# Lead-in of a fused retention and feed-forward kernel: k and q of units 1 to 3 loaded ahead of their V, V of units 1 and 2 scaled by GpSimd, tail tables made by products on VectorE

## The chip, the cores and the metric

The kernel runs on one core of a Trainium2 chip. The metric is the device time of one execution in microseconds (us); lower is better. Most executions of one kernel agree within about 0.3%, which is 0.9 us here.

TensorE is called PE below (the weight loads that overlap it PEld), VectorE is DVE, ScalarE is ACT, GpSimd is POOL. "L454" is line 454 of the kernel. The changed set-up functions are one line longer in all, so the lines after them (from L302 on) have a number one higher: L454 of the kernel before is L455 of the changed kernel. Some experiments shift them a little further.

## The reference, cut to what matters

```python
# q, k, v: (8 batches, 8 heads, 576 positions, 64), float32
scores = (q @ k.T) / sqrt(64)
gamma  = 1 - 2 ** (-5 - head)                 # one decay per head
ret    = scores * where(i >= j, gamma ** (i - j), 0)
x      = (ret @ v)  -> (4608, 512)            # heads side by side
h      = x @ w_in                             # (512, 2048)
out    = (h * sigmoid(1.702 * h)) @ w_out     # (2048, 512)
```

The kernel cuts the 4608 rows into 36 units of 128 rows. The decay `gamma ** (i - j)` is split into a factor of the row of q (table `gq`, applied when the result leaves PSUM, the memory that TensorE writes to) and a factor of the row of V (table `vfac`, applied to V before use). Earlier blocks of one batch enter through a running state (`kv`). For each unit TensorE transposes k and q and makes the scores; VectorE masks them (`pm`); "inter" is q times the running state, "values" the masked scores times the scaled V (`vp`), and both add up to the product that VectorE multiplies by `gq` into `xT`. Four units make one chunk of 512 rows for the feed-forward products. Unit 8 of each pair of batches holds both batches' last 64 rows ("tail") and needs its own rows of the two tables.

## The kernel before

Each engine has its own list of operations; a scheduler class puts in semaphore waits where one engine reads what another wrote. So the order of the calls below is the order on each engine. The first four units are written out by hand; this is the lead-in, which ends with the first up-projection (`up(0, 0)`, L454).

```python
def scale_v(u):                       # V times its decay factor, on VectorE
    sl, _, ty = u % NVN, *unit_info(u)[1:]
    op("dve", lambda e: e.tensor_tensor(
        vp[u % NVP].ap(), vn[sl].ap(),
        vfac[:, ty, :, None].to_broadcast([P, H, DH]), ALU.mult), ...)

def setup_last():                     # tables of the tail, as exponentials on ScalarE
    for hp in range(HP):
        op("act", ... gq[:, 4, hp, :] = Exp(iota_c[512:576] * lng + lnsc))
    # ... two small additions on VectorE ...
    for h in range(H):
        op("act", ... vfac[:, 4, h] = Exp(-log(gamma(h)) * iota_t))

# ... the lead-in ...
for i, src in enumerate((k, q)):      # unit 0: SyncE's queue
    op("sp", ... kq32[:, i, :] <- src[0, :, 0:P, :])
load_v(0, "sp")
setup_first(); setup_gq(0, 1); setup_gq(1, 4); setup_last()
for u in range(1, 4):                 # GpSimd's queue, in this order
    load_kq(u)                        # k, then q; float32 in DRAM, bf16 in SBUF
    load_v(u)                         # float32 to float32
for i in range(4):
    load_win(i)                       # w_in: 4 blocks, each 1 MB in DRAM
for u in range(4, 8):
    load_kq(u)
    load_v(u)
# ...
warm(10)                              # filler matmuls that keep PE busy
transpose_half(0, 0, "S2", "dve"); transpose_half(0, 1, "S3", "dve")
warm(3)
head_s(0)                             # scores on PE, two mask products on VectorE
scale_v(0); scale_v(1)
transpose_half(1, 0, "S2", "act")     # PE transposes k of unit 1, ScalarE copies
warm(4)
transpose_half(1, 1, "H0", "act")
head_k(0, "act")                      # state: PE, then two copies on ScalarE
head_v(0)                             # inter + values on PE, product xT on VectorE
head_s(1)
scale_v(2)
# ... unit 2 ...
head_k(1, "act"); head_s(2); scale_v(3); head_v(1)
# ... unit 3 ...
head_k(2, "act"); setup_gelu(); head_s(3); head_v(2); warm(3); head_v(3)
head_k(3, "act"); setup_tail()
warm(2)
play(16, lambda f: up(0, f), {9: [lambda: head_in(4, "dve")], ...})
```

`up(0, f)` reads `xT` of units 0 to 3 and block `f // 4` of `w_in`. `head_in(4)`, after ten of the sixteen up-projections, transposes k and q of unit 4.

## Time and profile before

| | |
|---|---|
| time, median of 3 runs | 312.8 us (312.46 to 312.85) |
| span of the profiled run | 311.03 us |
| PE busy | 301.9 us, 97% |
| first up-projection (L454) | starts at 19.72 us |
| last load of the lead-in (V of unit 3) | lands at 15.95 us |

The page of the profile first gives the busy time of each engine, and then slices of 1/40 of the span in tenths:

```profile
PE 301.9 (97%) x2169; PEld 155.7 (50%) x2169; DVE 134.5 (43%) x272; ACT 123.4 (40%) x225; POOL 105.6 (34%) x132
PE   6799999999999999999999999999999999999994
```

PE is full in all slices but the first two (15.5 us) and the last. The busy times of the other engines, 34 to 43%, say nothing of use: they are averages over stages. What can be gained is the time until the first up-projection, so one reads the chain of waits there. The chain is followed back from the last instruction; each line is a start, a length and what ran; "issue" is time for which the profile shows no wait, and `psS`, `psO`, `psH` are banks of PSUM. This is its part in the lead-in (cuts marked by dots):

```profile
7.16 1.70 POOL kq L203 x2
8.86 7.09 DMA vn<-in_v_dram
15.95 0.02 issue
15.98 0.69 DVE vp L302
16.67 0.60 DVE xT L443
17.27 0.60 DVE pm_0 L423
17.87 0.61 DVE pm_1 L423
18.48 0.04 issue
18.52 0.41 PE psO L433 x7
18.93 0.33 PE psS L347 x4
...
19.72 8.81 PE psH L454 x40
```

GpSimd issues loads (L203), the V of unit 3, issued at 8.86, lands at 15.95, then VectorE scales it (`vp`), finishes unit 1 (`xT`) and masks the scores of unit 3 (`pm`), then PE does the values of unit 3. The chain leaves one thing out. L454 also reads `xT`, and VectorE's timeline has the last two `xT` products end at 18.38 + 1.28 = 19.66, 0.06 before L454:

```profile
18.38 1.28 DVE L443 TENSOR_TENSOR xT<-psO,gq 128x512 bf16<-128x512 f32 x2
```

The chain follows PE's own earlier instructions there, because fillers kept PE from being idle.

### The profile page before, as it was taken

To read this page: it belongs to the slowest core of one execution; us is meant where nothing else is said; L and a number is where in the kernel's file an instruction comes from. 1 tells how busy PE (TensorE), PEld (TensorE's weight loads), DVE (VectorE), ACT (ScalarE), POOL (GpSimd) and SP (SyncE) were. 2 spreads that over 40 slices of the span, in tenths; PEclk is the share of its full clock that TensorE was granted. 3 is DMA by queue.
4 is the path that set the end of the run, shared out by engine and by line. 5 is a ranking of instruction groups with operands and counts; after the bars stand their busy time and mean duration, and the time that the engine had idled before them with its cause. 6 is when DMAs were issued, how large, how long until landed. Compare 5 with 4: busy or idle time off the path is not lost.

```text
span 311.0 us, 5149 instructions
## 1 busy us (share of the span) xinstructions
PE 301.9 (97%) x2169; PEld 155.7 (50%) x2169; DVE 134.5 (43%) x272; ACT 123.4 (40%) x225; POOL 105.6 (34%) x132
## 2 busy tenths in 40 slices
PE   6799999999999999999999999999999999999994
PEld 2444588655454545454545454545454545444441
DVE  5761984597445542545363625362627150100000
ACT  9666345301433333333333333333343434343411
POOL 9999923015699935334454300000000000000000
PEclk9999999999999999999999999999999999999999
DMA  9999999999999999999999999923210102010012
GB/s 150 184 207 188 190 203 175 176 187 157 182 118 200 168 163 150 170 135 176 179 141 190 145 148 182 142 47 86 45 68 2 67 2 67 2 67 34 36 67 67
DMA packets 113752, 39.40 MB, mean 127 GB/s; under 512 B 102785, under 2 KB 106881, under 8 KB 113729
## 3 DMA queue, kind: packets, MB, share of 16 engines
q0 software_dynamic: 80016, 22.55, 74.7%
q1 hardware_dynamic: 33712, 16.52, 30.9%
q8 instruction: 17, 0.28, 0.4%
q14 instruction: 7, 0.05, 0.1%
HBM read 36.70 MB, written 9.44 MB: 148 GB/s over the span
## 4 chain that ended last, share of the span: by engine, by line
PE 92%; POOL 3%; DMA 2%; DVE 2%; ACT 0%; issue 0%; POOLq 0%
PE psH L454 36%; PE psS L485 33%; PE psH L471 5%; PE psH L485 5%; PE psO L433 3%; PE psS L414 3%; DMA vn<-in_v_dram 2%; PE psS L347 2%; PE psO L485 2%; POOL kq L203 2%; PE psO L395 1%; PE psS L311 1%; POOL vn L217 1%; DVE vp L302 0%; DVE xT L443 0%; DVE pm_0 L423 0%
## 5 line engine op out<-in xcount | busy, mean ns | idle before, releaser
L454 PE MATMUL psH<-xT,w_in_sb 128*128 128x512 bf16 x512 | 127.3, 380 | 0.0
L459 ACT ACTIVATE gT<-psH 128x512 bf16<-128x512 f32 x128 | 76.4, 597 | 116.1 <-PE psH L454 116.1
L485 PE MATMUL psS<-w_out_sb,gT 128*128 128x512 bf16 x480 | 117.3, 379 | 0.0
L454 PEld LDWEIGHTS psH<-xT,w_in_sb 128*128 128x128 bf16 x512 | 47.8, 98 | 58.7 <-ACT gT L459 3.2
L485 PEld LDWEIGHTS psS<-w_out_sb,gT 128*128 128x128 bf16 x480 | 46.0, 98 | 51.7
L203 POOL DMA_DIRECT2D kq<-in_k_dram x39 | 35.6, 921 | 43.3 <-DMA qkT<-kq 22.7
L203 POOL DMA_DIRECT2D kq<-in_q_dram x39 | 35.5, 919 | 15.2 <-issue 15.2
L217 POOL DMA_DIRECT2D vn<-in_v_dram x39 | 36.0, 932 | 9.3 <-issue 5.0
L423 DVE TENSOR_TENSOR pm_0<-psS,mask 128x512 bf16<-128x512 f32 x32 | 22.0, 687 | 37.6 <-PE psS L414 37.5
L493 ACT ACTIVATE osb<-psS 128x512 f32<-128x512 f32 x30 | 17.9, 597 | 30.4 <-PE psS L485 30.4
L443 DVE TENSOR_TENSOR xT<-psO,gq 128x512 bf16<-128x512 f32 x36 | 23.5, 682 | 11.4 <-PE psO L433 11.4
L302 DVE TENSOR_TENSOR vp<-vn,vfac 128x512 bf16<-128x512 f32 x36 | 23.7, 685 | 2.6 <-DMA vn<-in_v_dram 2.5
L423 DVE TENSOR_TENSOR pm_1<-psS,mask 128x512 bf16<-128x512 f32 x32 | 21.8, 680 | 0.0
L377 DVE TENSOR_TENSOR kvf<-psS,kvf 64x256 f32<-64x256 f32 x24 | 10.1, 421 | 26.2 <-PE psS L347 26.0
L471 PE MATMUL psH<-xT,w_in_sb 128*128 128x256 bf16 x128 | 15.2, 273 | 0.0
L485 PE MATMUL psH<-w_out_sb,gT 128*128 128x512 bf16 x64 | 15.0, 380 | 0.0
L476 ACT ACTIVATE gT<-psH 128x512 bf16<-128x512 f32 x16 | 9.6, 597 | 11.5 <-PE psH L471 11.5
L414 PE MATMUL psS<-qkT 64*128 64x128 bf16 x288 | 12.2, 218 | 1.1 <-ACT qkT L330 0.9
L433 PE MATMUL psO<-pm_0,vp 128*64 128x128 bf16 x144 | 13.1, 224 | 0.0
L433 PE MATMUL psO<-pm_1,vp 128*64 128x128 bf16 x144 | 12.5, 223 | 0.5 <-DVE pm_1 L423 0.5
L471 PEld LDWEIGHTS psH<-xT,w_in_sb 128*128 128x128 bf16 x128 | 12.0, 98 | 1.9 <-issue 0.2
L375 DVE COPY kvf<-psS 64x256 f32<-64x256 f32 x12 | 5.0, 420 | 18.2 <-PE psS L347 18.1
(78 smaller groups left out, 171.9 us busy)
## 6 DMA issues: line engine op xcount, KB each, us to landing
out_dram<-osb SPq DMA_DIRECT2D x32, 256.0 KB, 3.1
vn<-in_v_dram POOLq DMA_DIRECT2D x31, 256.0 KB, 20.0
kq<-in_k_dram POOLq DMA_DIRECT2D x31, 128.0 KB, 21.4
kq<-in_q_dram POOLq DMA_DIRECT2D x31, 128.0 KB, 21.3
w_in_sb<-in_moe_w_in_dram POOLq DMA_DIRECT2D x4, 512.0 KB, 11.2
w_out_sb<-in_moe_w_out_dram POOLq DMA_DIRECT2D x4, 512.0 KB, 19.6
vn<-in_v_dram POOLq DMA_DIRECT2D x8, 128.0 KB, 23.1
out_dram<-osb SPq DMA_DIRECT2D x8, 128.0 KB, 4.3
```

Of the source, the lines that this page charges most:

```text
L203: e.dma_start(kq[sl][p0 : p0 + n, i, :].rearrange("p (h d) -> p h d", d=DH), src[b, :, s0 : s0 + n, :].rearrange("h p d -> p h d"),)
L217: e.dma_start(vn[sl][p0 : p0 + n, :, :], v[b, :, s0 : s0 + n, :].rearrange("h p d -> p h d"),)
L302: op("dve", lambda e: e.tensor_tensor(vp[u % NVP].ap(), vn[sl].ap(), vfac[:, ty, :, None].to_broadcast([P, H, DH]), ALU.mult), reads=[f"vn ...
L414: op("pe", lambda e, hp=hp, hh=hh, bank=bank: e.matmul(by_pair(bank)[:, hp, :], qt[64 * hh : 64 * hh + 64, hp, :], qt[64 * hh : 64 * hh + ...
L423: op("dve", lambda e: e.tensor_tensor(pm[u % 4][hh].ap(), by_pair(bank), m[:, None, :].to_broadcast([P, HP, P]), ALU.mult), reads=[bank, " ...
L433: op("pe", lambda e, hp=hp, hh=hh: e.matmul(ob[64 * hh : 64 * hh + 64, hp, :], vp[u % NVP][:, 2 * hp + hh, :], pm[u % 4][hh][:, hp, :], st ...
L443: op("dve", lambda e: e.tensor_tensor(xT[ch % 3][:, :, 128 * j : 128 * j + 128], by_pair(bank), gq[:, ty, :, :], ALU.mult), reads=[bank] + ...
L454: op("pe", lambda e, a=a: e.matmul(hb, w_in_sb[:, a, P * f : P * f + P], xT[c % 3][:, a, :], start=(a == 0), stop=(a == HP - 1)), reads=[f ...
L459: op("act", lambda e: e.activation(gT[c % 2][:, f, :], hb, AF.Gelu_apprx_sigmoid), reads=[bank], writes=[f"gT{c % 2}_{f}"])
L471: op("pe", lambda e, a=a, f=f, j=j: e.matmul(hb[:, j, :], w_in_sb[:, a, P * f : P * f + P], xT[c % 3][:, a, n], start=(a == 0), stop=(a == ...
L485: op("pe", lambda e, f=f: e.matmul(y, gT[c % 2][:, f, P * r : P * r + P], w_out_sb[:, f, :], start=(f == 0), stop=(f == NF - 1)), reads=[f ...
L493: op("act", lambda e: e.activation(osb[o].ap(), y, AF.Copy), reads=[bank], writes=[f"osb{o}"])
```

## The change

The intent is to shorten the lead-in: have the transposes and scores of units 1 to 3 done earlier by loading their k and q first, take two products off VectorE, which is on the chain, and take twelve exponentials off ScalarE. The diff, cut:

```diff
-        def setup_last():            # ... 12 exponentials on ScalarE, 2 additions ...
+        def setup_g64():
+            op("act", ... g64 = Exp(64 * lng))
         def setup_tail():
             ...
+            op("dve", ... gq[:, 4] = gq[:, 3, :, 64:128] * g64)
+            for h in range(H):
+                for hh in range(2):
+                    op("dve", ... vfac[64*hh : 64*hh+64, 4, h] =
+                              vfac[64*hh : 64*hh+64, 3, h] * gamma(h) ** (64.0*hh - 128.0))
-        def scale_v(u):
+        def scale_v(u, eng="dve"):
-        setup_last()
-        for u in range(1, 4):
-            load_kq(u)
-            load_v(u)
-        for i in range(4):
-            load_win(i)
+        setup_g64()
+        load_kq(1)
+        load_kq(2)
+        load_v(1)
+        load_kq(3)
+        load_v(2)
+        load_v(3)
+        load_win(0)
+        load_win(1)
+        scale_v(1, "pool")
+        load_win(2)
+        scale_v(2, "pool")
+        load_win(3)
@@ order of the lead-in's work, the new order from unit 1 on @@
+        head_v(0)
+        transpose_half(2, 0, "S2", "act")
+        head_s(1)
+        transpose_half(2, 1, "H0", "act")
+        head_k(0, "act")
+        warm(1)
+        head_s(2)
+        transpose_half(3, 0, "S2", "act")
+        inter(1); values(1); values_out(1)
+        transpose_half(3, 1, "H0", "act")
+        head_k(1, "act")
+        warm(1)
+        head_s(3)
+        scale_v(3)
+        warm(2)
+        head_k(2, "act")
+        head_v(2)
+        setup_gelu()
+        inter(3); values(3); values_out(3)
+        head_k(3, "act")
+        setup_tail()
```

More of the change, by code (lines that the diff above doesn't have):

```diff
@@ L167, in bass_retnet_parallel__then__act_gelu_quick_kernel @@
         iota_k = sb("iota_k", [P, 4], FP32)
-        iota_t = sb("iota_t", [P, 1], FP32)
+        g64 = sb("g64", [P, HP], FP32)
         scr = sb("scr", [P, 1], FP32)
@@ L268, in setup_gq @@
                    writes=[f"gq{hp}_{c}" for c in range(c0, c1)])
-        def setup_last():
-            for hp in range(HP):
-                op("act", lambda e, hp=hp: e.activation(
-                    gq[:, 4, hp, :].rearrange("p (t i) -> p t i", i=64),
-                    iota_c[:, None, 512:576].to_broadcast([P, 2, 64]),
-                    AF.Exp, bias=lnsc.ap(), scale=lng[:, hp : hp + 1]),
-                   reads=["iota_c", "lnsc", f"lng{hp}_0", f"lng{hp}_1"], writes=[f"gq{hp}_4"])
-            op("dve", lambda e: e.tensor_scalar_add(iota_t[0:64], iota_k[0:64, 0:1], 512.0),
-               reads=["iota_k"], writes=["iota_t0"])
-            op("dve", lambda e: e.tensor_scalar_add(iota_t[64:128], iota_k[64:128, 0:1], 448.0),
-               reads=["iota_k"], writes=["iota_t1"])
-            for h in range(H):
-                op("act", lambda e, h=h: e.activation(
-                    vfac[:, 4, h : h + 1], iota_t.ap(), AF.Exp, scale=-math.log(gamma(h))),
-                   reads=["iota_t0", "iota_t1"], writes=[f"vfact{h}"])
+        def setup_g64():
+            op("act", lambda e: e.activation(g64.ap(), lng.ap(), AF.Exp, scale=64.0),
+               reads=[f"lng{hp}_{hh}" for hp in range(HP) for hh in range(2)], writes=["g64"])
         def setup_gelu():
@@ L295, in setup_tail @@
                 op("dve", lambda e, j=j: e.memset(kv[1][j].ap(), 0.0), writes=[f"kv1_{j}"])
+            op("dve", lambda e: e.tensor_tensor(
+                gq[:, 4, :, :].rearrange("p a (t i) -> p a t i", i=64),
+                gq[:, 3, :, None, 64:128].to_broadcast([P, HP, 2, 64]),
+                g64[:, :, None, None].to_broadcast([P, HP, 2, 64]), ALU.mult),
+               reads=["g64"] + [f"gq{hp}_3" for hp in range(HP)],
+               writes=[f"gq{hp}_4" for hp in range(HP)])
+            for h in range(H):
+                for hh in range(2):
+                    op("dve", lambda e, h=h, hh=hh: e.tensor_single_scalar(
+                        vfac[64 * hh : 64 * hh + 64, 4, h : h + 1],
+                        vfac[64 * hh : 64 * hh + 64, 3, h : h + 1],
+                        gamma(h) ** (64.0 * hh - 128.0), ALU.mult),
+                       reads=[f"vfac{h}"], writes=[f"vfact{h}_{hh}"])
         VF = [f"vfac{h}" for h in range(H)]
-        VFT = [f"vfact{h}" for h in range(H)]
-        def scale_v(u):
+        VFT = [f"vfact{h}_{hh}" for h in range(H) for hh in range(2)]
+        def scale_v(u, eng="dve"):
             sl, _, ty = u % NVN, *unit_info(u)[1:]
-            op("dve", lambda e: e.tensor_tensor(
+            op(eng, lambda e: e.tensor_tensor(
                 vp[u % NVP].ap(), vn[sl].ap(),
@@ L630, in bass_retnet_parallel__then__act_gelu_quick_kernel @@
         scale_v(0)
-        scale_v(1)
         transpose_half(1, 0, "S2", "act")
@@ L634, in bass_retnet_parallel__then__act_gelu_quick_kernel @@
         transpose_half(1, 1, "H0", "act")
+        head_v(0)
+        transpose_half(2, 0, "S2", "act")
+        head_s(1)
+        transpose_half(2, 1, "H0", "act")
         head_k(0, "act")
-        head_v(0)
-        head_s(1)
-        scale_v(2)
-        transpose_half(2, 0, "S2", "act")
-        warm(2)
-        transpose_half(2, 1, "H0", "act")
-        head_k(1, "act")
-        head_s(2)
-        scale_v(3)
-        head_v(1)
-        transpose_half(3, 0, "S2", "act")
-        transpose_half(3, 1, "H0", "act")
+        warm(1)
+        head_s(2)
+        transpose_half(3, 0, "S2", "act")
+        inter(1)
+        values(1)
+        values_out(1)
+        transpose_half(3, 1, "H0", "act")
[3 more added lines that the diff above has]
+        scale_v(3)
+        warm(2)
         head_k(2, "act")
+        head_v(2)
         setup_gelu()
-        head_s(3)
-        head_v(2)
-        warm(3)
-        head_v(3)
+        inter(3)
+        values(3)
+        values_out(3)
         head_k(3, "act")
```

## The prediction

> **What bounds it now.** The page gives TensorE (PE) 301.9 of 311.0 us (97%); the chain that ended last is 92% PE. From 20 us on PE is nearly full (windows: 2.00 of 2.00 us in each from 20 to 36). PE work is unchanged but for fewer filler matmuls, so only the lead-in can change: the time to the first up-projection (L454) at 19.72 us (PE timeline). The chain there: GpSimd issues loads back to back (0.88 us each), V of unit 3 lands at 15.95, then four VectorE ops of 0.6 us (scale V 3, xT of unit 1, two mask products of unit 3), then values, states and filler on PE.
>
> **What the change does.**
> - Load order. Landings (semaphores): k1 7.73, q1 9.03, v1 10.32, k2 11.20, q2 12.04, v2 13.33, k3 14.21, q3 15.04, v3 15.95. A k or q costs about 0.86, a V 1.3. In the new order: k2 9.9, q2 10.8, v1 12.0, k3 12.9, q3 13.8, v2 15.0, v3 still about 16.0, as the bytes are the same.
> - V of units 1 and 2 leave VectorE (0.69 us each). On GpSimd, an estimate from the Trainium skill (GPSIMD Engine Reference, Performance versus the Vector engine: a 2048-wide tensor_tensor 4497 ns, VectorE 2293): about 1.2 us for 512. They hold GpSimd's queue, so w_in 2 and 3 and all after are issued up to 4.5 us later; but the queue is 14 us deep there (w_in 3 issued 11.95, landed 25.88), so landings should not move.
> - ScalarE loses 12 exponentials (L272 1.63 us, L282 0.84 us), gains one: the first kT copy goes at 8.2 instead of 9.02. Not on the chain, which waits for loads.
> - VectorE gains one 128x512 product and 16 tiny ones (about 2 us) after the last xT, where it idles 7.9 us. Free.
>
> **New chain.** v2 lands 15.0; GpSimd to 16.3; state 2 on PE to 16.65; its ScalarE copies (0.76) to 17.45; inter and values of unit 3 to 18.1; xT 3 on VectorE to 18.8; first L454 at 18.9. The mask products of unit 3 and xT 1 are done before. Gain at L454 about 0.8 us, out of the 3.8 us that followed v3.
>
> **What caps it.** Unit 4's transposes come 8.6 us after the first L454. q4 landed 27.76 and is used at 28.58: slack 0.8 us, so more gain than that is lost there. The first w_in block (18.18) has 0.7 us.
>
> **Prediction.** 312.8 - 0.7 = 312.1 us, 8 in 10 between 311.5 and 312.7. Faster by over 2%: 0.01; within 2%: 0.97; slower by over 2%: 0.02.
>
> **What would show it.** First L454 near 18.9; v2 landing near 15.0, v3 near 16.0; GpSimd TENSOR_TENSOR near 1.2 us; the chain of waits in the lead-in passing through GpSimd's product of unit 2 and the kv_2 copy instead of VectorE's mask products; q4 landing still near 27.8, with a short PE wait at unit 4's transposes; everything after shifted alike.
>
> **What would make it wrong.** A GpSimd product of 2 us eats the gain one for one. VectorE and GpSimd contending: the skill (SBUF — State Buffer, Who interferes with whom) says a VectorE op with two SBUF inputs and a GpSimd op that reads SBUF block each other; scale V 3 starts about when the second product ends. Late issue of w_in 3 leaving a hole in the load queue would move every later landing. Fewer fillers might let the PE clock drop (granted 1.00 now).

## More of the kernel before

The runs were made in four sessions; in each, the kernel before was run beside the others on the same chip, and times are only compared within a session.

## The result, and the profile after

Ratios are the mean time of one kernel's runs over that of the other's runs of the same rounds, so they are not quite the ratio of the medians that are quoted beside them.

| | before | changed |
|---|---|---|
| median of 5 runs | 312.85 us (312.46 to 313.25) | 312.69 us (312.36 to 313.00) |
| ratio | | 0.9994 (95%: 0.998 to 1.0007) |
| span of the profiled run | 311.03 | 310.65 |
| first up-projection | 19.72 | 19.33 |

The time lies in the predicted range (311.5 to 312.7) at its upper edge, and the ratio by itself doesn't tell a gain from none. The profile tells more. These are the same lines of the page:

```profile
PE 302.3 (97%) x2168; PEld 155.9 (50%) x2168; DVE 136.6 (44%) x285; ACT 121.6 (39%) x214; POOL 108.1 (35%) x134
PE   7799999999999999999999999999999999999994
```

And this is the chain of waits in the lead-in:

```profile
8.08 7.21 DMA vn<-in_v_dram
15.29 0.08 issue
15.37 1.04 POOL vp L303
16.41 0.14 issue
16.55 0.40 PE psS L348 x4
...
16.97 0.38 ACT kv_2 L361
...
17.36 0.39 ACT kv_2 L361
...
17.80 0.40 PE psO L396 x4
18.19 0.34 PE psO L434 x8
18.54 0.33 PE psS L348 x4
...
19.33 8.81 PE psH L455 x40
```

The chain is the one that the prediction wrote down: V of unit 2 lands, GpSimd multiplies it, PE makes the state, ScalarE copies it in two pieces, PE does inter and values of unit 3. VectorE's `xT` of unit 3, 18.58 to 19.27, again stands beside the last PE lines:

```profile
18.58 0.69 DVE L444 TENSOR_TENSOR xT<-psO,gq 128x512 bf16<-128x512 f32 x1 [0.24 <-PE psO L434]
```

VectorE's mask products are gone from the chain. The first up-projection is 0.39 us earlier, and the first down-projection is 0.38 us earlier (57.06 against 57.44), so in this pair of profiles what the lead-in gains goes through to the end.

So the mechanism holds in this trace, but 0.39 is half of the predicted 0.8, and the timed runs show 0.2. Is the gain real, what sets its size, and which part of the change gives it?

### The profile page after: what moved, and what is told of

It is laid out like the page before. It is cut to its first block, busy times and chain, and to the rows that moved or that the text cites. A ratio compares the mean times of both kernels' runs of the same rounds, so it can differ in the third digit from the quotient of the medians.

```text
span 310.7 us, 5152 instructions
## 1 busy us (share of the span) xinstructions
PE 302.3 (97%) x2168; PEld 155.9 (50%) x2168; DVE 136.6 (44%) x285; ACT 121.6 (39%) x214; POOL 108.1 (35%) x134
## 4 chain that ended last, share of the span: by engine, by line
PE 92%; POOL 2%; DMA 2%; DVE 1%; ACT 0%; issue 0%; POOLq 0%
PE psH L455 36%; PE psS L486 33%; PE psH L472 5%; PE psH L486 5%; PE psO L434 3%; PE psS L415 3%; PE psS L348 2%; DMA vn<-in_v_dram 2%; PE psO L486 2%; POOL kq L203 2%; PE psO L396 2%; PE psS L312 1%; POOL vp L303 0%; PE psO L403 0%; ACT kv_2 L361 0%
## 5 line engine op out<-in xcount | busy, mean ns | idle before, releaser
L455 PE MATMUL psH<-xT,w_in_sb 128*128 128x512 bf16 x512 | 127.3, 379 | 0.0
L455 PEld LDWEIGHTS psH<-xT,w_in_sb 128*128 128x128 bf16 x512 | 47.9, 98 | 58.7 <-ACT gT L460 3.2
L203 POOL DMA_DIRECT2D kq<-in_k_dram x39 | 36.3, 945 | 48.1 <-DMA qkT<-kq 23.6
L203 POOL DMA_DIRECT2D kq<-in_q_dram x39 | 36.3, 937 | 7.4 <-issue 7.4
L303 DVE TENSOR_TENSOR vp<-vn,vfac 128x512 bf16<-128x512 f32 x34 | 22.4, 686 | 1.8 <-DMA vn<-in_v_dram 1.6
L378 DVE TENSOR_TENSOR kvf<-psS,kvf 64x256 f32<-64x256 f32 x24 | 10.1, 421 | 26.5 <-PE psS L348 26.3
L348 PE MATMUL psS<-vp,kq 128*128 128x128 bf16 x128 | 12.4, 220 | 0.2 <-POOL vp L303 0.2
```

The costliest lines, as they stand in the source:

```text
L203: e.dma_start(kq[sl][p0 : p0 + n, i, :].rearrange("p (h d) -> p h d", d=DH), src[b, :, s0 : s0 + n, :].rearrange("h p d -> p h d"),)
L303: op(eng, lambda e: e.tensor_tensor(vp[u % NVP].ap(), vn[sl].ap(), vfac[:, ty, :, None].to_broadcast([P, H, DH]), ALU.mult), reads=[f"vn{s ...
L348: op("pe", lambda e, hp=hp: e.matmul(kb[:, hp, :], kq[sl][:, 0, P * hp : P * hp + P], vp[u % NVP][:, 2 * hp : 2 * hp + 2, :], start=(first ...
L455: op("pe", lambda e, a=a: e.matmul(hb, w_in_sb[:, a, P * f : P * f + P], xT[c % 3][:, a, :], start=(a == 0), stop=(a == HP - 1)), reads=[f ...
```

## The experiments

The theories, by the letters that the texts use:

- A: the chain above sets the start of the up-projection. Then load order and order of work give the gain; tables and ScalarE's relief give nothing; GpSimd's product lies on the chain with its full length.
- B: ScalarE's exponentials held the lead-in, and GpSimd's product has slack.
- C: the 0.39 us is scatter of the loads; there is no gain.
- D: taking V off VectorE is what gains.
- E: the order of loads is worth nothing, since the last byte lands at the same time.

Since the gain is smaller than the scatter of whole runs, one more reading was needed. The loads of GpSimd's queue land one after another, and in different profiles of kernels with the same first loads the whole queue is early or late: q of unit 1 landed between 8.23 and 9.53 us. Measured from that landing, the same kernel repeats within 0.1 us. This table was worked out from the semaphore times in the traces; all columns but the first two are us after q of unit 1 landed. "last xT" is the end of VectorE's `xT` of unit 3; the up-projection can start 0.06 later if the first block of `w_in` is there. In bold: a first block that landed late, and an up-projection that it held.

| profile of | q1 landed at (us) | V 2 | first w_in block | last xT | first up-projection |
|---|---|---|---|---|---|
| before | 9.03 | +4.30 | +9.16 | +10.64 | +10.69 |
| tables only | 9.18 | +4.29 | +9.17 | +10.60 | +10.66 |
| old load order | 8.98 | +4.30 | +9.15 | +10.81 | +10.87 |
| changed, first | 9.20 | +6.09 | +9.28 | +10.07 | +10.13 |
| changed, second | 8.98 | +6.10 | **+10.60** | +10.07 | **+10.73** |
| changed, third | 9.53 | +6.01 | +9.13 | +9.99 | +10.05 |
| GpSimd's product twice | 8.30 | +5.96 | **+10.41** | +10.95 | +11.01 |
| q4 earlier | 8.69 | +6.09 | **+10.32** | +10.07 | **+10.46** |
| V 2 on VectorE | 9.08 | +6.09 | +9.24 | +9.81 | +9.86 |
| V 1 and 2 on VectorE | 8.23 | +6.05 | **+10.36** | +9.77 | **+10.49** |
| swap | 8.47 | +6.11 | +9.34 | +9.68 | +9.73 |
| swap, q4 earlier | 8.59 | +6.09 | +9.33 | +9.74 | +9.80 |
| the same again | 8.50 | +6.10 | **+10.33** | +9.70 | **+10.46** |
| best | 8.49 | +6.09 | +8.13 (half a block) | +9.63 | +9.69 |

What follows the first up-projection can be compared in the same way. Lined up there, all 14 profiles run alike to the end of the span, 291.32 us later, but for two kinds of loss. One is a late q of unit 4 or of a later unit (below). The other lies near 70 us, where "tables only", "old load order" and "GpSimd's product twice" lost 0.33, 0.44 and 0.27 us and "changed, third" 0.06. The first up-projection plus 291.32 us plus these losses gives each profiled span within 0.03 us. So a gain at the first up-projection does reach the end; but the profiled runs of those three kernels also hold a loss that has nothing to do with the lead-in, and their timed ratios have to be read with that in mind.

### The tables alone

The kernel before, with `setup_last` replaced by `setup_g64` and the products in `setup_tail`, nothing else:

```diff
-        setup_last()
+        setup_g64()
         for u in range(1, 4):
             load_kq(u)
             load_v(u)
```

> The kernel before with one part of the change alone: the tail tables by products on VectorE. Theory A: nothing, since ScalarE's first kT copy (9.02) moves to about 8.3 but the chain waits for V 3 at 15.95: first up-projection 19.6 to 19.9, time within 0.1 us of before. Rival B (ScalarE's exponentials held the lead-in): first up-projection near 19.3, 0.4 us faster.

Measured: median 312.73 us, ratio 0.9990 (0.9975 to 1.0004). The first up-projection came at 19.84, on the same chain as before:

```profile
16.10 0.69 DVE vp L303
16.80 0.60 DVE xT L444
17.40 1.21 DVE pm L424 x2
```

The last xT lies at +10.60 against +10.64. The tables give nothing that can be told from zero, and theory B falls in its first half. The ratio alone would not have settled it; the chain does.

### GpSimd's product made twice

```diff
         load_win(2)
+        op("pool", ... junk = vn2 * vfac)     # the same product into a spare tile
         scale_v(2, "pool")
         load_win(3)
```

> The changed kernel with GpSimd's product of unit 2 made twice (the first into a spare tile), 1.04 us more on GpSimd. Theory A: the chain passes through it, so the first up-projection moves by 1.0 us to about 20.3 and the time by 1.0 us to about 313.6. Rival B (the product has slack): under 0.3 us. A third reading: w_in 3 and all later loads are issued 1 us later, but they should land where they did (w_in 3 near 26.1, q4 near 28.0).

Measured: median 312.95 us, ratio 1.0007 (0.9985 to 1.0029). The chain of its profile:

```profile
14.27 0.08 issue
14.35 1.03 POOL junk L614
15.38 1.02 POOL vp L304
16.40 0.14 issue
16.54 0.40 PE psS L349 x4
```

The queue happened to be early in this profile (q1 at 8.30), so the first up-projection stands at 19.31 and not at the expected 20.3; a reader who compared only that number would call theory A wrong. Counted from the landing of V 2, it is 5.04 us (14.27 to 19.31) against 4.04 in the changed kernel (15.29 to 19.33): one whole product more, as theory A says. The rest of theory B falls. In time it is 0.0025 above the changed kernel's ratio of that session (0.9982), about 0.8 us of 312.9, but the two intervals overlap, one of the four runs (314.47 us) makes most of it, and the profiled run lost 0.27 us near 70 us; so the time proves nothing here. q4 landed at 27.86, so GpSimd's delayed issues moved no landing.

### V of unit 2, then of both, back on VectorE

```diff
         load_win(2)
-        scale_v(2, "pool")
         load_win(3)
...
         head_k(1, "act")
+        scale_v(2)
         warm(1)
         head_s(3)
```

> The changed kernel with V of unit 2 scaled on VectorE again (placed before the mask products of unit 3), V of unit 1 still on GpSimd. VectorE stood idle from 14.98 to 15.78 there. Theory A: vp 2 is ready at about 15.95 instead of 16.4 plus a 0.14 handover, the mask products of unit 3 end 0.2 later, and the chain now goes over VectorE: first up-projection about 19.1, 0.2 to 0.3 us under the changed kernel. If VectorE is what binds (each op it gives up is gained), it is slower than the changed kernel: 19.6 or later.

Measured: median 312.34 us, ratio 0.9979 (0.9967 to 0.9991). The chain is VectorE's again:

```profile
15.17 0.02 issue
15.19 0.69 DVE vp L303
15.89 1.20 DVE pm L424 x2
17.08 0.61 DVE vp L303
17.70 0.04 issue
17.74 0.41 PE psO L434 x8
```

The last xT comes 0.26 us earlier than in the changed kernel (+9.81 against +10.07), as expected. In time nothing of it is seen: the changed kernel's median in that session is 312.36 us, its ratio 0.9982. In the second kernel unit 1's V went back too:

```diff
-        scale_v(1, "pool")
...
         head_k(0, "act")
+        scale_v(1)
         warm(1)
         head_s(2)
```

> The changed kernel with V of units 1 and 2 both back on VectorE (unit 1's before the mask products of unit 2, unit 2's before those of unit 3): load order, order of work and tables as changed, nothing on GpSimd. Theory A (the gain comes from the load order with the order of work, and GpSimd's product is a slower stretch of the last chain): as the run with only unit 2 back: first up-projection 18.9 to 19.1, 0.5 to 0.7 us under before. Rival D (taking V off VectorE is what gains): 19.6 or later, no gain left.

Measured: median 312.11 us against 312.69 for the kernel before in that session, ratio 0.9987 (0.9975 to 0.9999). The last xT lies at +9.77, as with one product back. Theory D falls: with nothing on GpSimd the work of the lead-in is done not later but 0.3 us earlier than in the change. (The timed runs don't show these 0.3 us; the changed kernel was not in that session.) A GpSimd product costs 1.03 to 1.04 us with 0.08 before and 0.14 after it; VectorE's costs 0.69, and VectorE stood idle for 0.79 us just before the mask products of unit 3.

This profile shows a second thing, in a line of PE's timeline (start, length, what; in brackets the idle time before and what ended it):

```profile
18.72 0.59 PE L455 MATMUL psH<-xT,w_in_sb 128*128 128x512 bf16 x2 [0.70 <-DMA w_in_sb<-in_moe_w_in_dram]
```

All of xT was ready at 18.00, but the first block of `w_in` landed at 18.58. So here the loads of `w_in` are the next limit.

### The old load order

```diff
-        load_kq(1)
-        load_kq(2)
-        load_v(1)
-        load_kq(3)
-        load_v(2)
-        load_v(3)
+        for u in range(1, 4):
+            load_kq(u)
+            load_v(u)
```

> The changed kernel with the loads of units 1 to 3 in the old order (k, q, V unit by unit). V 2 lands near 13.4 again and GpSimd's two products are early, but q3 lands near 15.1: scores of unit 3 near 16.2, its mask products to 17.6, then scale V 3, values, xT. Theory A: first up-projection near 19.5, so most of the gain is gone (0 to 0.2 us under before) and the chain has no GpSimd in it. Rival E (the order of loads is worth nothing, as the last byte lands at the same time): 19.3 or earlier, gain kept.

Measured: median 312.91 us, ratio 1.0005 (0.9991 to 1.002); first up-projection 19.86. Both times of the expectation were a little too good (19.5 expected), the direction was right: with the old order of loads the whole gain is gone. Theory E falls. The last bytes do land at the same time (V 3 at 15.91 against 15.95 to 16.40), but q of unit 3 lands at 14.99 instead of 13.9 to 14.4, and from it hangs a longer string of work than from any V: 4.87 us to the first up-projection (14.99 to 19.86), against 4.04 from V 2 and 3.77 from V 3 (15.95 to 19.72 before). This is the chain from there:

```profile
15.18 0.34 PE psH L326 x4
15.53 0.02 issue
15.55 0.60 ACT qkT L331
16.16 0.14 issue
16.29 0.40 PE psS L415 x8
16.69 0.54 PE psH L508 x2
17.23 0.24 PE psS L348 x4
```

Transpose, copy, scores, fillers, state: nothing that GpSimd does is in it. Two things in the 4.87 us are not work that needs q: PE took q's transposes 0.19 us after the landing, since it was still busy with values (the view follows the chain over these to k of unit 3, landed at 14.17), and 0.54 us are fillers. The fillers alone don't explain the loss, since VectorE, which has no fillers, ends its string from the same scores (two mask products, then V 3) at 18.59, about 0.1 before PE takes the values of unit 3. What the new load order would give with the old order of work was not tried; so the gain belongs to the two together.

### The changed kernel twice more

> The changed kernel once more, unaltered, for the scatter. Theory A (the lead-in's last chain is V of unit 2 landing, GpSimd product, state on PE, kv_2 copy on ScalarE, inter and values of unit 3, xT of unit 3): the first L455 comes 4.0 us after V 2 lands whatever the landing is (15.29 to 19.33 in the first profile), so 19.1 to 19.5 if the landing scatters by 0.25; time 0.2 to 0.5 us under before. Rival C (the 0.38 us in the first profile was scatter of the loads): the first L455 near 19.7 and a ratio of 1.000.

Measured: median of 6 runs 312.36 us, ratio 0.9982 (0.9969 to 0.9995). A third session:

> The changed kernel a third time, unaltered, because its first two ratios (0.9994 and 0.9982) lie a whole gain apart. Theory A: L455 is set by the later of V 2's landing plus 4.04 us and the first w_in block's landing plus 0.14: 19.0 to 19.7, against about 19.8 before; the ratio of the three pooled is 0.998 to 0.999, 0.3 to 0.6 us. Rival C: 1.000.

Measured: 312.39 us, ratio 0.9983 (0.9971 to 0.9996). Theory C falls, on two grounds: two of three intervals exclude 1, and counted from q1 the last xT is 0.53 to 0.65 us earlier in all three profiles of the changed kernel than in the two with the old chain. The second is the stronger one, as "tables only", whose chain is unchanged, has a ratio of 0.9990. The mean of the three ratios is 0.9986, which is 0.43 us of 312.9.

The two profiles show why a run can have the gain or lose it. The third one is the first again (V 2 at 15.54, first up-projection 4.04 us later at 19.58). The second one, whose run at 313.07 us was the slowest of its six, reads:

```profile
19.72 0.38 PE L455 MATMUL psH<-xT,w_in_sb 128*128 128x512 bf16 x1 [0.63 <-DVE maskc L279]
```

The releaser named here, a table of VectorE, is wrong: L455 doesn't read it. It is just the last semaphore event before the start. The trace's semaphore of the first `w_in` block was complete at 19.58, and L455 started 0.14 later, the same 0.14 as in the runs where the view names that load (18.58 to 18.72 above, 19.02 to 19.16 below). So this run had xT ready at 19.06, as early as theory A says, and lost 0.6 us to a load. Then q of unit 4 landed at 28.78 and cost another 0.25 (the first down-projection came 37.98 us after the first up-projection, 37.73 in the first profile).

### k and q of unit 4 ahead of the last w_in block

```diff
         scale_v(2, "pool")
+        load_kq(4)
         load_win(3)
-        for u in range(4, 8):
-            load_kq(u)
-            load_v(u)
+        load_v(4)
+        for u in range(5, 8):
+            load_kq(u)
+            load_v(u)
```

> The changed kernel with k and q of unit 4 ahead of the last w_in block (q4 lands near 25.3 instead of 27.9, w_in 3 near 27.9, needed near 29.7). In a run whose loads are on time q4 is no wait in the changed kernel (27.98 against use at 28.19), so theory A: the same L455 and a median within 0.15 us of the changed kernel's, with the slow runs (a loss at q4 as in the second profile, 0.43 us) gone. If q4 is what the prediction called a cap in most runs: 0.3 us faster than the changed kernel.

Measured: median 312.31 us, ratio 0.9985 (0.9972 to 0.9999), beside 0.9983 for the changed kernel in the same session: no difference. The wait in this profile is again for `w_in`:

```profile
19.16 0.38 PE L455 MATMUL psH<-xT,w_in_sb 128*128 128x512 bf16 x1 [0.37 <-DMA w_in_sb<-in_moe_w_in_dram]
```

So q4, which the prediction named as the cap, doesn't hold the changed kernel when its loads are on time: in the first and third profile it has 0.2 us to spare (`w_in` has 0.7 to 0.8). Where the first block of `w_in` is late, as here, that block holds the up-projection. Its slowest run was 312.92 us and the changed kernel's 312.75, so the expected loss of slow runs wasn't seen either.

### Better placements

In "swap", V 2 is on VectorE and V 3 on GpSimd:

```diff
         load_win(2)
-        scale_v(2, "pool")
         load_win(3)
+        scale_v(3, "pool")
...
+        scale_v(2)
         warm(1)
         head_s(3)
-        scale_v(3)
```

> The changed kernel with GpSimd's second product moved from unit 2 to unit 3: V 1 and V 3 on GpSimd, V 2 on VectorE. V 3 lands near 16.05, GpSimd to 17.1 plus 0.14, mask products of unit 3 to 17.1 on VectorE at the same time, so values of unit 3 start near 17.3 to 17.7: theory A: first up-projection 18.5 to 18.8, 0.8 us under before at most, unless the first w_in block (lands 18.3 to 18.5) or q4 (lands 27.9, then needed near 27.4 to 27.7) holds it: 0.2 to 0.5 us of PE wait at unit 4's transposes.

Measured: 312.49 us, ratio 0.9996 (0.9984 to 1.0009), with runs from 311.82 to 313.10, the widest spread of the session. The profiled run was the fastest of the six and shows the wait for q4 that was expected:

```profile
27.40 0.40 PE L312 MATMUL psS<-ident,kq 128*128 128x128 bf16 x4 [0.17 <-DMA kq<-in_q_dram]
```

The bracket understates it, since ends of matmuls are modelled: lined up at the first up-projection, all that follows is 0.34 us later than in the changed kernel, and another 0.14 are lost near 50 us.

The next kernel is swap with `load_kq(4)` placed before `load_win(3)`:

> The run before (V 3 on GpSimd, V 2 on VectorE) with k and q of unit 4 loaded ahead of the last w_in block, so that q4 lands near 25.3 and w_in 3 near 27.9 (needed near 29). Theory A with the cap: the wait at unit 4's transposes is gone; total 0.8 to 1.0 us under before, 0.2 to 0.4 under the run before. If the cap was no cap: equal to the run before within 0.1 us.

Measured: 311.87 us, ratio 0.9977 (0.9965 to 0.9989), and no wait at unit 4. By the ratios of the two, the early q4 is worth 0.0019, 0.6 us; the next run says to take that with care. It was run once more in the last session:

> The best run so far once more (V 2 on VectorE, V 3 on GpSimd, k and q of unit 4 ahead of the last w_in block): L455 4.9 us after q3 lands or with the first w_in block, 18.4 to 18.8; 0.7 us under before, and 0.3 to 0.5 under the changed kernel on the same chip.

Measured: 312.70 us, ratio 0.9988 (0.9975 to 1.0): half of the gain only, and nothing that could be told from the changed kernel (0.9983). In its profile all of xT was ready at 18.20 and the first `w_in` block landed at 18.83, so the same load cost 0.7 us again. This expectation failed. For the other four runs, which were slower than the profiled one (312.05 us), the reason is not shown.

The last kernel starts from that one, drops three fillers, and loads the first `w_in` block in two halves, so that the products of the first half can start earlier:

```diff
-        load_win(0)
+        load_win0(0)          # columns 0 to 255
+        load_win0(1)          # columns 256 to 511
...
         head_s(3)
-        warm(2)
         head_k(2, "act")
...
-        warm(2)
+        warm(1)
         play(16, lambda f: up(0, f), {
```

> The run before with the two filler matmuls between the scores of unit 3 and the state of unit 2 taken out (0.54 us of PE in the chain of that run), one filler less before the up-projection, and the first w_in block loaded in two halves so that its first half lands 1.2 us earlier. Theory A: L455 at 18.0 to 18.5, another 0.2 to 0.4 us: 0.9 to 1.1 us under before. If the PE clock needs the fillers, the first 10 us of up-projections run at half speed and it is slower than before.

Measured: 311.97 us (311.88 to 312.47), ratio 0.9972 (0.9959 to 0.9984), 0.9 us under the kernel before: the fastest of the kernels that were run beside it, ahead of both the kernel before and the changed one. The first half of `w_in` landed at 16.62, the up-projection started at 18.18 as soon as xT was there. The fillers were not missed: the up-projections ran at 8.81 us for 40, as before. Now the next load shows, q of unit 5:

```profile
31.07 0.40 PE L321 MATMUL psS<-ident,kq 128*128 128x128 bf16 x4 [0.39 <-DMA kq<-in_q_dram]
```

It makes all that follows 0.56 us later. Fillers and halves were changed together and ran in one session; what each is worth wasn't tried.

## Why the prediction was right or wrong

**The bound and the place: right.** PE is full from 20 us on, and a gain at the first up-projection goes through to the end, as long as the next loads allow it: 0.39 us there, 0.38 at the first down-projection and in the span (311.03 to 310.65).

**The new chain: right, link by link.** Landing of V 2, GpSimd, state, two copies, inter and values, xT. The product made twice moved the end of that chain by 1.00 us after V 2's landing.

**The tables and ScalarE's relief: right, free and worth nothing.** Ratio 0.9990 with 1 in its interval, the same chain. The size of what VectorE gained was off: about 2 us predicted, 3.2 measured (0.62 for the wide product, 2.56 for the sixteen tiny ones), in idle time.

**Landings not moved by GpSimd's late issues: right.** `w_in` 3 was issued at 16.36 instead of 11.95 and landed at 26.12 instead of 25.88; the whole queue of that run was already 0.2 late at q1.

**The size: too large.** Predicted 0.7 us, measured 0.43 as the mean of three sessions (0.2 in the first). That the first session's 312.69 us fell inside the range, by 0.01, was luck; the 312.36 and 312.39 of the later ones lie well inside. Two terms failed.

- "V 2 lands 15.0; ... first L454 at 18.9. Gain at L454 about 0.8 us". Counted from q1's landing, which takes out the scatter, the first up-projection came 10.69 and 10.66 us later in the two profiles with the old chain, and 10.13 and 10.05 in the two profiles of the changed kernel where no load held it: a gain of 0.58. V 2 lands 0.04 to 0.13 later after q1 than predicted (6.01 to 6.10, predicted 5.97). The chain from there takes 4.04 us instead of 3.9: GpSimd was as predicted (0.08 + 1.04 + 0.14 = 1.26, predicted 1.3), but state (0.40 instead of 0.35), and inter and values up to the start of xT (17.80 to 18.58, 0.78 instead of 0.65) took longer.
- "The first w_in block (18.18) has 0.7 us." This treated a landing as fixed, read from one profile. In 8 of the 13 profiles with whole `w_in` blocks the first block landed 9.1 to 9.3 us after q1; in 5 it landed 10.3 to 10.6 after. The up-projection can start 0.14 after the landing. The kernel before starts it at 10.69, so a late block would cost it next to nothing. The changed kernel can start at 10.1, so in the late case the block holds the up-projection (two profiles: 10.73 in the changed kernel and 10.46 in the one with q4 earlier) and nearly all of the gain goes. With 8 and 5 of 13 as weights, an estimate of the gain is (8 x 0.58 + 5 x 0.08) / 13 = 0.39 us, which is about the 0.43 measured. The weights are from profiled runs of several kernels, so this is an estimate and not a proof: all five late cases are among the ten profiles with the new load order, and with these ten alone the estimate is 0.33 us.

**The cap at q4: right, but not reached by this change.** In the first and third profile q4 landed 0.2 us before its use (27.98, used at 28.19), so the predicted short wait didn't show: the lead-in gained less than q4's slack. In the second profile q4 was late and cost 0.25 us. In kernels with a shorter lead-in q's transposes began 0.05 us after its landing, and what was gained beyond the slack was lost, as predicted: 0.09 us with V 2 on VectorE (first up-projection at 18.94), 0.19 with V 1 and 2 (18.72), 0.34 in swap (18.20, q4 landing 0.4 us earlier).

**Contention and the PE clock: not seen in the changed kernel.** GpSimd's products took 1.03 to 1.04 us and V 3's product on VectorE 0.68, as before the change, because it began only at 16.99, after GpSimd's second product ended at 16.41. With the product made twice the two did overlap, and VectorE's took 0.97 (from 15.97 on, GpSimd's until 16.39); it wasn't on the chain there. The granted clock reads 0.998 instead of 1.000, because the clock's record has half speed from 309.2 us on; the last matmul ended at 306.7.

What the prediction didn't ask is whether GpSimd's part was needed. It isn't: in the traces it delays the last xT by about 0.3 us.

What stays open: why the first `w_in` block lands 1.0 to 1.5 us later in some runs. The loads before it don't share it (V 3 is on time); the second block is still late (12.2 to 12.8 us after q1 instead of 11.6 to 11.9). No view shows which of the 16 DMA engines was late. Four of the five late cases had q1 landing early (8.23 to 8.69; so had two cases without it), and none of the three profiles with the old load order has a late block, so it isn't excluded that the new load order brings it about. The cause of the losses near 70 us stays open too.

## What to carry to other kernels

When loads come from one full queue, ask for each load how much work hangs from its landing, and put the ones with the longest string first; the landing of the last byte says little. A gain in such a lead-in eats the cushion of the next load: read for every later load by how much it beats its use, and how far landings scatter between runs, since a cushion below the scatter turns part of the gain back into waits. Where an effect is smaller than the scatter of whole runs, measure it in the trace from an event that both kernels share, and let the timed rounds only confirm the sum.

## What the Trainium skill lacked or had wrong

- GPSIMD Engine Reference, Performance versus the Vector engine: it gives 4497 ns against 2293 for a 2048-wide two-input float32 product, a ratio of 1.96. Here a 512-wide one with bf16 result took 1035 ns on GpSimd and 690 on VectorE, a ratio of 1.5; the prediction's 1.2 us was 16% too long, a plain quarter of the page's figure (1.12 us) 9%. Width and type differ, so this doesn't contradict the page's figure. The page doesn't give the handover: 0.08 us before the product and 0.14 after it.
- SBUF — State Buffer, Who interferes with whom: its rule that a VectorE operation with two SBUF inputs contends with a GpSimd operation that reads SBUF agrees with the one overlap in these runs: with the product made twice, V 3's product on VectorE, begun while GpSimd's ran, took 972 ns instead of 682, and GpSimd's 1034 as without it. The small 128x128 mask on VectorE (`maskc`), which has one input in SBUF, took between 0.22 and 0.71 us from one profile to another while GpSimd was issuing loads, and casts of the state near 69 us took 0.29 us in the first changed profile, where GpSimd issued nothing then, and up to 0.70 in others, where it issued loads. Contention of the kind that the page describes would fit; no run here isolates it.
- DMA: Bandwidth & Descriptors: I found nothing there on how far landings scatter between runs of one program. Here the same first loads landed at 8.23 to 9.53 us, and the first `w_in` block either 9.1 to 9.3 or 10.3 to 10.6 us after them. That scatter is larger than the effect of the change.
- TensorE: Matmul & The Clock Gate, The HAM clock gate: it says that the window runs freely and that the change to full speed varies by 500 ns either way. In the 14 profiles here full speed began at 4.16 to 6.78 us, a wider spread, with the same ten fillers from 1.19 us on; the fastest profiled run (311.50 us) had the latest change.
